# Attention resumes at the first unfinished step: absent parts of a batch's first chunk count as done

## The chip, the core and the metric

The kernel runs on one core of a Trainium2 chip. The metric is the time of one execution on the device in microseconds (us). TensorE is called PE here, VectorE DVE, ScalarE ACT, GpSimd POOL and SyncE SP.

## What is computed

Three layers follow each other: a gated linear attention with a running state per head, a dense two-layer MLP, and a mixture of eight experts of which each token takes one.

```python
# attention: 4 batches, 8 heads, 768 steps, head size 40
m_new = np.maximum(f_gate[:, :, t] + m, i_gate[:, :, t])
C = f_stab[:, :, None, None] * C + i_stab[:, :, None, None] * np.einsum('bhd,bhe->bhde', vt, kt)
h_tilde = np.einsum('bhde,bhe->bhd', C, qt)
denom = np.maximum(np.abs(nq), 1.0)
y[:, :, t] = o * h_tilde / denom
# dense layer: 3072 tokens, 320 -> 2048 -> 320
x = (np.maximum(x @ w_in, 0.0) ** 2) @ w_out
# routed layer: 8 experts, 320 -> 1024 -> 320, gate_w from a softmax
out[mask] = gate_w[mask, None] * (np.maximum(x[mask] @ w1[e], 0.0) @ w2[e])
```

## The kernel before

**Attention in chunks.** The sequence of each batch is cut into 6 chunks of 128 steps (`c` is the chunk's place in its batch, 0 to 5), 24 chunks in all. Chunks 0 to 2 are the first ones (c = 0) of batches 0 to 2; then come chunks 3 to 7 (batch 0, c = 1 to 5), 8 to 12 (batch 1), 13 to 17 (batch 2) and 18 to 23 (batch 3). A chunk's work is a list of named parts in nine steps (`STEPS`): scores q·k (`scores`, L775), the product of q with the carried state C (`inter`, L715), the weighting by decays (`weigh0`, `weigh1`, L780), the products with v (`values0`, `values1`, L788), the new state (`update`, L715, and `update_masked`, `carried`, L811 to L819), the division, the gate, and a transpose into the layout of the dense layer (`turned`, L724). For c = 0 there is no carried state, so `inter`, `scaled` and `carried` issue nothing there.

**Loads and preparation.** `prepare(n, h)` runs ahead of a chunk: loads of kvo (L616), of q and k (`st`, L629, 960 KB a chunk, two buffers), of decays (L650), all on SP's queue; the rounding of q and k (ACT L640, POOL L643, four pieces a half) and the causal mask of the decays (POOL L671, L672).

**Dense layer in groups.** Three chunks are a group of 384 tokens; there are 8 groups. Each group takes 16 iterations (f): eight matmuls of layer 1 (L866) and nine of layer 2 (L899 to L901). Layer 1 runs two iterations ahead of layer 2. A group's sums leave PSUM at L981; `fin` then computes the experts' logits of that group (L955, L964) and writes the tokens out (L1059, on SP) in steps, one an iteration.

**What sets the order.** The order is written by the program that builds the kernel. First it goes through a list of words, `PLAN`, that interleaves the attention of chunks 0 to 6, the decoding of the dense weights and the first iterations, one word at a time. The list ends after layer 1 of iteration 17 and layer 2 of iteration 15, that is at the end of group 0, with chunks 0 to 6 through all their parts. Behind it a loop over iterations takes over. Each iteration calls `attend` twice; `attend` adds 0.7 to a counter and for each whole number runs one `half` step: the due tail step (`rest`), the next step of `steps[0]` (six a chunk, `PERIOD`) and its `prepare`. A part that is in `done` is not issued again. `half` stops at `evac(first[g1 + 2])`, a limit of two groups ahead. Before layer 1 of a new group, `until` runs all `half` steps at once that this group still needs.

**Where the loop starts.** `catch_up` moves `steps[0]` past the steps whose parts are all in `done`, and calls `prepare` for them. `PLAN` has no word for `inter`, `scaled` and `carried` of chunks 0 to 2, so step 0 of chunk 0 is never finished by that test, and `steps[0]` stays 0. The loop then spends 42 half steps (7 chunks of 6) on parts that are all done.

Of the kernel before, what the change touches and what calls it, by code (L numbers as in the profile page):

```python
# [373 lines left out]
def kernel(ctx, tc, qk, q3, kvo, gates, w_io, wg, w12, cst, out, dbg=None):  # L374
# [361 lines left out]
    class Main:  # L736
# [18 lines left out]
                self.run(part)  # L755

        def finished(self, k):
            return all(part in self.done for part in self.STEPS[k])

        def inter(self):  # L760
            d = self.d
# [788 lines left out]
```

## Time and profile before

| | us |
|---|---|
| median of 3 runs (824.13 to 825.09) | 824.89 |
| the profiled execution | 822.93 |
| its span, first to last instruction | 821.1 |
| PE busy in the span | 777.9 |
| DVE, ACT, POOL busy | 503.5, 407.7, 384.8 |
| group 1, from the end of group 0 to its own | 84.27 |
| groups 2, 3, 4, 5 | 65.35, 65.63, 60.45, 63.41 |
| groups 6, 7 | 50.76, 48.97 |

A group's time is read between the starts of its and the preceding group's evacuation (L981). Busy times of PE are of pipelined matmuls whose ends are modelled. A page has 40 slices of 20.5 us; the granted clock of PE is 1.00 at 2.4 GHz and 0.50 at 1.2 GHz. The profiled execution took 1.96 us less than the median.

### The profile page before, as it was taken

The page shows a single profiled execution, that of the slowest core. Times are in us where ns is not written, and L with a number is a line of the kernel's source. Part 1 is how long each engine was busy: PE and PEld are TensorE (multiplying, and loading weights), DVE is VectorE, ACT ScalarE, POOL GpSimd, SP SyncE. Part 2 cuts the span into 40 slices and gives each one's busy share as a digit, 9 for nine tenths or more (in the row PEclk, how much of TensorE's full clock was granted, in tenths as well). Part 3 has the DMA queues.
Part 4 walks back from the last instruction along what each step waited for, and adds up shares of the span by engine and source line. Part 5 has one row for each costly group of instructions (what it writes and reads, how often), then busy time and mean ns, then how long its engine had stood idle before and what let it go on. Part 6 is the DMA issues. An engine that isn't in the chain of part 4 may idle for free.

```text
span 821.1 us, 14163 instructions
## 1 busy us (share of the span) xinstructions
PE 777.9 (95%) x5120; PEld 753.8 (92%) x5120; DVE 503.5 (61%) x1102; ACT 407.7 (50%) x760; POOL 384.8 (47%) x430
## 2 busy tenths in 40 slices
PE   7999999995899989999999999999989999999996
PEld 5789989995899989899999999999989999999996
DVE  6358998454458567748558655444527555886553
ACT  2346766332445544454454543454327544876553
POOL 5238997017555665554454410142044533465551
PEclk9999999995799999999999999999989999999998
DMA  8257861046485445454343400010048666777520
GB/s 260 79 159 220 235 177 31 1 135 169 111 269 151 122 117 149 107 141 122 87 121 109 143 1 31 2 47 13 31 126 303 197 184 181 206 248 231 192 70 32
DMA packets 55046, 109.03 MB, mean 133 GB/s; under 512 B 6896, under 2 KB 34681, under 8 KB 54834
## 3 DMA queue, kind: packets, MB, share of 16 engines
q1 hardware_dynamic: 50370, 95.88, 40.1%
q0 software_dynamic: 4160, 11.77, 4.4%
q8 instruction: 48, 0.79, 0.4%
q10 hardware_dynamic: 432, 0.29, 0.1%
q14 instruction: 36, 0.29, 0.1%
HBM read 98.69 MB, written 10.86 MB: 133 GB/s over the span
## 4 chain that ended last, share of the span: by engine, by line
PE 63%; POOL 8%; DVE 8%; DMA 6%; issue 3%; ACT 1%; SPq 1%; DVEq 0%; POOLq 0%; ACTq 0%
PE hp L866 16%; PE hp L288 12%; DMA st<-in_qk_dram 6%; PE acc L899 5%; PE acc L901 5%; PE acc L900 5%; PE op L308 3%; PE op L307 3%; PE op L309 3%; POOL kq L643 3%; PE pv L788 2%; POOL Ab L671 2%; PE lp L964 1%; PE xp L274 1%; PE tp L715 1%
## 5 line engine op out<-in xcount | busy, mean ns | idle before, releaser
L643 POOL TENSOR_TENSOR kq<-st,kq 120x256 fp32r<-120x256 f32 x136 | 100.3, 769 | 101.7 <-ACT kq L640 90.1
L899 PE MATMUL acc<-w_h,gh 128*128 128x320 f32 x384 | 125.7, 327 | 0.0
L901 PE MATMUL acc<-w_h,gl 128*128 128x320 f32 x384 | 120.0, 313 | 1.5 <-POOL gl L886 1.4
L866 PE MATMUL hp<-xh,w_h 128*128 128x384 f32 x384 | 114.4, 352 | 5.9 <-ACT scr L959 2.0
L900 PE MATMUL acc<-w_l,gh 128*128 128x320 f32 x384 | 119.3, 311 | 0.0
L874 ACT ACTIVATE g<-hp 128x384 f32<-128x384 f32 x128 | 62.0, 484 | 105.5 <-PE hp L866 104.9
L883 DVE SCALAR_TENSOR_TENSOR hp<-hp,g 128x384 f32<-128x384 f32 x121 | 67.7, 559 | 66.5 <-ACT g L874 66.3
L257 DVE SCALAR_TENSOR_TENSOR gl<-hp,gh 128x384 fp32r<-128x384 f32 x88 | 47.1, 553 | 71.2 <-ACT gh L227 59.3
L866 PE MATMUL hp<-xh,w_l 128*128 128x384 f32 x384 | 89.0, 340 | 0.2 <-POOL w_l L582 0.2
L866 PE MATMUL hp<-xl,w_h 128*128 128x384 f32 x256 | 87.8, 343 | 0.0
L886 DVE TENSOR_TENSOR gl<-hp,gh 128x384 fp32r<-128x384 f32 x121 | 67.5, 558 | 13.4 <-DVE hp L883 0.5
L901 PEld LDWEIGHTS acc<-w_h,gl 128*128 128x128 f32 x384 | 73.0, 190 | 2.0 <-POOL gl L886 1.7
L866 PEld LDWEIGHTS hp<-xh,w_h 128*128 128x128 f32 x384 | 66.8, 192 | 8.2 <-ACT scr L959 2.3
L899 PEld LDWEIGHTS acc<-w_h,gh 128*128 128x128 f32 x384 | 73.3, 191 | 0.1
L900 PEld LDWEIGHTS acc<-w_l,gh 128*128 128x128 f32 x384 | 73.4, 191 | 0.0
L866 PEld LDWEIGHTS hp<-xh,w_l 128*128 128x128 f32 x384 | 70.2, 191 | 0.5 <-POOL w_l L582 0.5
L875 ACT ACTIVATE gh<-g 128x384 fp32r<-128x384 f32 x128 | 67.2, 525 | 6.0 <-PE acc L900 2.0
L227 ACT ACTIVATE gh<-hp 128x384 fp32r<-128x384 f32 x88 | 42.6, 491 | 44.9 <-PE hp L288 43.6
L678 ACT ACTIVATE Ab<-Ab 128x512 f32<-128x512 f32 x42 | 26.2, 628 | 70.8 <-POOL Ab L672 70.7
L640 ACT ACTIVATE kq<-st,cs 120x1024 fp32r<-120x1024 f32 x34 | 38.9, 1145 | 44.6 <-DMA st<-in_qk_dram 42.7
L684 POOL TENSOR_TENSOR vw<-kvo,wT 128x378 f32<-128x378 f32 x20 | 17.2, 858 | 86.5 <-DMA kvo<-in_kvo_dram 36.1
L788 PEld LDWEIGHTS pv<-kvo,Ab 128*128 128x128 f32 x384 | 55.5, 218 | 1.6 <-DVE Ab L780 1.5
(273 smaller groups left out, 1929.2 us busy)
## 6 DMA issues: line engine op xcount, KB each, us to landing
st<-in_qk_dram SPq DMA_DIRECT2D x34, 480.0 KB
raw<-in_w_dram SPq DMA_DIRECT2D x30, 512.0 KB
kvo<-in_kvo_dram SPq DMA_DIRECT2D x24, 529.0 KB
raw<-in_w_io_dram SPq DMA_DIRECT2D x16, 704.0 KB
Ab<-A_d SPq DMA_DIRECT2D x42, 256.0 KB
raw<-in_w_dram SPq DMA_DIRECT2D x20, 427.0 KB
raw<-in_w_dram SPq DMA_DIRECT2D x10, 426.0 KB
q<-in_q_dram SPq DMA_DIRECT2D x20, 180.0 KB
```

Of the source, the lines that this page charges most:

```text
L257: e.scalar_tensor_tensor(out=gl[:, j], in0=hp[j % 4], scalar=0.0, in1=gh[:, j].bitcast(F32), op0=ALU.max, op1=ALU.subtract).then_inc(sGL, 1)
L288: m = e.matmul(hp[f % 4][:, 0:w], a, c, start=(n == 0), stop=(n == 7))
L643: nc.gpsimd.tensor_tensor(out=o[:, c], in0=self.st[j][:, c], in1=o[:, c].bitcast(F32), op=ALU.subtract)
L788: nc.tensor.matmul(self.pv[:, hd], d.Ab[r][:, i], d.v[:, hd], start=True, stop=True)
L866: nc.tensor.matmul(hp, a, x, start=(n == 0), stop=(n == 7))
L874: nc.scalar.activation(out=r, in_=hp, func=ACTF.Relu)
L875: nc.scalar.activation(out=gh, in_=r, func=ACTF.Square)
L883: e.scalar_tensor_tensor(out=sq, in0=hp, scalar=0.0, in1=r, op0=ALU.max, op1=ALU.mult)
L886: e.tensor_tensor(out=gl, in0=sq, in1=gh.bitcast(F32), op=ALU.subtract)
L899: nc.tensor.matmul(acc[t][:, 0:DM], gh[:, sl], wh, start=(f == 0), stop=False)
L900: nc.tensor.matmul(acc[t][:, 0:DM], gh[:, sl], wl, start=False, stop=False)
L901: nc.tensor.matmul(acc[t][:, 0:DM], gl[:, sl], wh, start=False, stop=end)
```

## The change

`finished` takes `inter`, `scaled` and `carried` as done where c is 0. `catch_up` then moves `steps[0]` on to the first step that has something left.

```diff
@@ -755,7 +755,7 @@
         def finished(self, k):
-            return all(part in self.done for part in self.STEPS[k])
+            return all(part in self.done or (self.c == 0 and part in ("inter", "scaled", "carried")) for part in self.STEPS[k])
```

No instruction's form or operands change; the order does. On PE, behind the end of `PLAN` in group 1, the first two rows of chunk 7 (`tp<-C` is `inter`, `sp<-kq` is `scores`) now stand in the first iteration of the loop:

```order
 L866 MATMUL hp<-xl,w_h 128x384
 L866 MATMUL hp<-xh,w_l 128x384 x3
+L715 MATMUL tp<-C,q_1096 128x126 x3
+L775 MATMUL sp<-kq 128x128 x8
 L955 MATMUL lpt<-cs,xr_81 128x128 x3
 L899 MATMUL acc<-w_h,gh 128x320
```

Chunks 8 and 9 follow in later iterations of group 1 in the same way. Before, PE has these three chunks in one block between the last layer-1 products of group 1 and the first of group 2 (q_1096, q_1758 and q_1815 are the q of chunks 7, 8 and 9):

```order
L901 MATMUL acc<-w_h,gl 128x320
L715 MATMUL tp<-C,q_1096 128x126 x3
L775 MATMUL sp<-kq 128x128 x8
L788 MATMUL pv<-kvo,Ab 128x42 x8
L715 MATMUL tp<-C,q_1758 128x126 x3
L775 MATMUL sp<-kq 128x128 x8
L724 MATMUL xpt<-cs,kvo 128x128 x3
L715 MATMUL tp<-vw,kvo 120x126 x3
L788 MATMUL pv<-kvo,Ab 128x42 x8
L715 MATMUL tp<-C,q_1815 128x126 x3
L775 MATMUL sp<-kq 128x128 x8
L724 MATMUL xpt<-cs,kvo 128x128 x3
```

This block is gone from that place. On SP's queue, the loads of chunks 8, 9 and 10 now stand ahead of the writes of group 0's tokens (`x_d`); before, those of chunk 8 came behind them. SP, from the loads of chunk 9 on (q_1441 and q_1671 are the q of chunks 9 and 10 in the changed kernel):

```order
+L650 DMA Ab<-A_d 128x4x128 x2
+L616 DMA kvo<-in_kvo_dram 128x1058
+L629 DMA st<-in_qk_dram 120x1024 x2
+L633 DMA q_1441<-in_q_dram 120x384
+L650 DMA Ab<-A_d 128x4x128 x2
+L616 DMA kvo<-in_kvo_dram 128x1058
+L629 DMA st<-in_qk_dram 120x1024 x2
+L633 DMA q_1671<-in_q_dram 120x384
 L1059 DMA x_d<-xr_81 128x392 x3
 L650 DMA Ab<-A_d 128x4x128 x2
-L629 DMA st<-in_qk_dram 120x1024 x2
-L633 DMA q_1758<-in_q_dram 120x384
```

What moved is when SP may ask for q and k: the writes no longer stand in front of chunks 8 to 10.

Attention matmuls by group, counted from the order on PE between the last layer-2 products of one group and of the next (matmuls of `scores`, of `inter` and `update` together, of `values`, of `turned`; one call of a part is 8, 3, 4 and 3 matmuls):

| group | before | after |
|---|---|---|
| 1 | 24, 15, 24, 6 | 32, 21, 28, 9 |
| 2 | 32, 21, 24, 12 | 24, 15, 28, 9 |
| 3 | 24, 18, 32, 9 | 24, 18, 24, 9 |
| 4 | 24, 12, 24, 9 | equal |
| 5 | 24, 18, 24, 9 | equal |
| 6 | 8, 3, 8, 6 | equal |
| 7 | 0, 0, 0, 9 | equal |

## Rows read from the trace of the kernel before

**Rows 1.** The page: span, and slices of PE and its clock.
```profile
span 821.1 us, 14163 instructions
PE   7999999995899989999999999999989999999996
PEclk9999999995799999999999999999989999999998
```

**Rows 2.** Windows, groups 1 to 7: stretch, length, busy times (count), PEclk, DMA, GB/s.
```profile
136.30:220.57 84.27, 71.84 (x423) 69.25 (x422) 40.65 (x109) 30.99 (x60) 32.37 (x49) 0.80 0.32 87
220.57:285.92 65.35, 63.33 (x445) 61.88 (x443) 44.51 (x110) 33.39 (x67) 34.27 (x48) 1.00 0.64 190
285.92:351.55 65.63, 62.01 (x434) 60.64 (x434) 46.05 (x111) 31.91 (x64) 37.62 (x51) 1.00 0.44 120
351.55:412.00 60.45, 59.35 (x416) 58.66 (x415) 37.50 (x94) 30.21 (x60) 30.10 (x42) 1.00 0.43 117
412.00:475.41 63.41, 60.27 (x420) 59.10 (x419) 42.08 (x103) 30.62 (x61) 31.46 (x43) 1.00 0.42 119
475.41:526.17 50.76, 50.76 (x343) 50.52 (x342) 27.74 (x80) 20.26 (x45) 0.77 (x4) 1.00 0.04 13
526.17:575.14 48.97, 48.97 (x355) 48.62 (x353) 22.83 (x71) 24.11 (x49) 18.35 (x15) 1.00 0.08 26
```

**Rows 3.** Windows inside group 1, same columns.
```profile
136.30:178.40 42.10, 42.10 (x280) 41.69 (x279) 23.30 (x74) 16.78 (x36) 3.12 (x11) 1.00 0.19 56
178.40:210.60 32.20, 19.78 (x94) 17.59 (x93) 13.24 (x30) 10.74 (x17) 20.95 (x28) 0.56 0.55 145
210.60:220.57 9.97, 9.96 (x51) 9.97 (x52) 4.11 (x7) 3.47 (x8) 8.31 (x11) 0.72 0.14 29
200.00:210.00 10.00, 4.48 (x19) 3.61 (x18) 2.83 (x8) 2.56 (x6) 4.31 (x6) 0.50 0.75 190
217.00:219.00 2.00, 2.00 (x16) 2.00 (x15) 0.00 (x0) 0.00 (x0) 1.93 (x3) 1.00 0.40 75
```

**Rows 4.** Timeline of PE in the block: start, length, instruction, idle before, releaser.
```profile
186.68 2.74 PE L775 MATMUL sp<-kq 120*128 120x128 f32 x8 [1.80 <-POOL kq L643]
193.03 0.88 PE L724 MATMUL xpt<-cs,kvo 128*128 128x128 f32 x3 [3.61 <-DVE kvo L840]
205.60 0.88 PE L724 MATMUL xpt<-cs,kvo 128*128 128x128 f32 x3 [3.61 <-DVE kvo L840]
210.61 0.98 PE L866 MATMUL hp<-xh,w_h 128*128 128x384 f32 x2 [1.72 <-DVE xh L734]
```

**Rows 5.** Waits of SP's queue, 120 to 230 us: total, times, longest.
```profile
SPq L1059 <- DVE xr L1055: 40.9, 1, 40.9
```

**Rows 6.** Chain that ended last, full clock: start, length, attention products.
```profile
218.44 0.82 PE pv L788 x8
223.70 0.67 PE tp L715 x6
224.37 0.85 PE sp L775 x8
226.68 0.33 PE xpt L724 x3
```

**Rows 7.** The same chain: from a chunk's loads to its last mask, twice.
```profile
273.09 0.37 SPq L650
...
292.00 0.65 POOL Ab L672
...
310.39 0.39 SPq L650
...
329.98 0.65 POOL Ab L672
```

**Rows 8.** Waits, 220 to 480 us, and PE's longest idle time there.
```profile
ACT kq L640 <- DMA st<-in_qk_dram: 37.2, 11, 6.5
421.78 0.62 PE L866 MATMUL hp<-xh,w_h 128*128 128x384 f32 x2 [1.44 <-ACT scr L959]
```

## The prediction

> **What bounds the kernel now.** I read the page first: its slices of PE and of the granted clock [rows 1]. PE is at 9 nearly everywhere, so the kernel is bound by PE, with one clear exception: the tenth and eleventh slice (about 185 to 226 us) show PE at 5 and 8 tenths and the clock at 5 and 7. The second view is the windows by group [rows 2]. Group 1 takes 84.27 us, groups 2 to 5 take 60.45 to 65.63. The third is the same view inside group 1 [rows 3]. From 136.30 to 178.40 PE is busy all of 42.10 us at full clock, with POOL at 3.12 and DMA at 0.19: this is the dense layer alone, while the loop spends its half steps on chunks that are done. From 178.40 to 210.60 PE is busy 19.78 of 32.20 us at a mean clock of 0.56: this is the block of chunks 7, 8 and 9, which `until` issues at once. From 210.60 to 220.57 PE is busy, but at 0.72.
>
> The fourth view is the timeline of the block [rows 4]. PE stands 1.80 us for the rounding of q and k, twice 3.61 us for the end of the chunk before (DVE L840) and 1.72 us for the columns of group 2. In the block nothing lies beside these chains of load, rounding, mask, weighting and division, because no dense product is left to issue. The clock goes down with it: it is 0.50 (1.2 GHz) in the stretch 200 to 210 with PE busy 4.48 of 10 us, and 1.00 (2.4 GHz) again in 217 to 219 [rows 3].
>
> **The change, part by part.** *What PE must do.* The change adds and removes no products on PE; it moves them. I price them at full clock [rows 6]: a call of scores 0.85 us, of `inter` or `update` 0.67, of `values` 0.82, of `turned` 0.33. The dense part of a group comes from group 6, which holds little attention: 50.76 us [rows 2], less one call of scores, one of `inter`, two of `values` and two of `turned` (0.85 + 0.67 + 1.64 + 0.66 = 3.82), is 46.94 us.
>
> Before, by the counts of the change's table: group 1 has 3 scores, 5 products with the state, 6 values, 2 turned: 2.55 + 3.35 + 4.92 + 0.66 = 11.48, with the dense part 58.4 us. Groups 2 to 5 come to 61.3, 61.1, 58.1 and 59.4 in the same way. Against the measured 84.27, 65.35, 65.63, 60.45 and 63.41 [rows 2] the excess is 25.9 in group 1 and 4.1, 4.6, 2.4 and 4.0 in the others.
>
> After: group 1 has 4, 7, 7, 3 calls (3.40 + 4.69 + 5.74 + 0.99 = 14.8), 61.8 us; group 2 has 3, 5, 7, 3, 59.6 us; group 3 has 3, 6, 6, 3, 59.4 us. The sum of groups 1 to 3 is 180.8 us in both kernels; it is the excess that differs.
>
> *What the excess becomes.* Before it is 25.9 + 4.1 + 4.6 = 34.6 us in these three groups. In groups 2 to 5 the loop already runs as it will in group 1: steps of a chunk between dense products. Their mean excess is 3.7 us, from 2.4 to 4.6. I take it for each of the three groups after, 11.2 us with the decimals kept. The gain is 34.6 - 11.2 = 23.4 us. With 2.4 a group it is 27.4, with 4.6 a group 20.8.
>
> *What hides the moved work.* The DVE, ACT, POOL and DMA work of chunks 7 to 9 then lies beside group 1's dense products. In 136.30 to 178.40 DVE is busy 23.30, ACT 16.78 and POOL 3.12 of 42.10 us [rows 3], so there is room; over a whole group DVE would come to the 46 of 65.6 us that group 3 shows [rows 2]. Were that cover gone, the block's excess would come back, 25.9 - 3.7 = 22.2 us.
>
> *The queue of SP.* Before, SP stands 40.9 us for group 0's tokens (L1059 waits for DVE L1055) [rows 5], and the loads of chunk 8 stand behind it. After, the loads of chunks 8 to 10 come first. That is needed for the gain: chunk 8's scores now fall in group 1. The writes themselves come later. Their buffer is written again only at the end of group 2, a group's 65 us away, and the rows are read after group 5; I cost them at nothing. Behind them now stand kvo of chunk 10 and the decays, q and k of chunk 11. The writes' DVE part is issued in about the eleventh iteration of group 1, and so are these loads (15 half steps at 1.4 an iteration), so the wait should be short. The bounds are 0 and one iteration, about 65/16 = 4 us; I take 0, since in groups 2 to 5 the queue has the same order and its cost is in their 3.7.
>
> *POOL, ACT, DVE.* They run the same operations in another order. POOL, nearly idle while the dense layer runs alone and the feeder of the block behind it [rows 3], works through the whole group. Nothing is priced here beyond the excess. Nor are groups 4 to 7 and the routed layer: their order is the same, they start earlier, and PE is what they wait for.
>
> The sum: 822.93 us for the profiled execution less 23.4 is 799.5. The median stands 1.96 us above that execution, so on the median it is 824.89 - 23.4 = 801.5 us.
>
> **The rivals.** *First, the clock falls inside group 1 as well.* The block shows what a fall costs: a gap of 3.61 us [rows 4], and from 210.61 on, with PE busy, some 6.4 us at half speed until it is full in the window that starts at 217 [rows 3], so 3.2 us lost: 6.8 us a fall. One fall gives 808.3, two 815.1 us. Against it: groups 2 to 5 have 13 chunks' scores between dense products and show 1.00 throughout [rows 2], and PE's longest idle time there is 1.44 us [rows 8]. If each of the four calls of scores in group 1 brought a fall, it would be 4 x 6.8 = 27.2 us, 828.7 us in all; this decides from 23.4/6.8 = 3.4 falls on. I give it 1 in 100, and one or two falls 9 in 100. The Trainium skill, page "TensorE: Matmul & The Clock Gate", section "HAM oscillation — how this bites in real kernels", speaks against the change here: it describes a kernel whose waits for data return in each pass of its loop and put the clock down in each, so that the cost is paid every time and not once. By that rule the one fall of the block would become one for each chunk, the 828.7 us; the trace does not bear it out, since the clock row of groups 2 to 5 shows no fall.
>
> *Second, on the slower side: the chain of loads sets the pace.* The next q and k can be loaded only when the last have been rounded (two buffers), and ACT stands in its order until they land: 37.2 us in 11 waits [rows 8], with the dense ReLU behind it, and PE behind that. From a chunk's decay load to its last mask the chain takes 273.09 to 292.65, 19.6 us, and 310.39 to 330.63, 20.2 us [rows 7]. Group 1 takes 14 iterations of 1.4 half steps, 19.6 steps or 3.27 chunks. At 20.2 us a chunk that is 66.1 us, as much as the 61.8 + 3.7 = 65.5 that PE would take; the chain just fits. At 24 us a chunk group 1 would take 78.5, and the kernel 814.5 us. It is slower than before only from (65.5 + 23.4)/3.27 = 27.2 us a chunk on; at 30 us a chunk, with DMA, SP and POOL all late for each, it would be 834. For it: DMA is at 0.75 of its 16 engines in the window from 200 to 210 us, where the block waits for its loads [rows 3]; against it: 20 us is measured with the same loads in flight. 3 in 100 for slower, 8 in 100 for a loss of 5 to 13 us in this way.
>
> *Third, nothing changes:* the loop would reach the same limits by group 2 and lose what it gained, 824.9 us. The limit `evac` lets attention run two groups ahead, and before it is caught up by group 3 in any case; so the products move within groups 1 to 3 only. But what is gained is PE's idle and half-speed time, and it would have to come back as new idle time in a later group whose order is the same. 3 in 100.
>
> *Fourth, more than forecast:* the excess of groups 2 and 3 was the block's aftermath, and all three groups come to their products alone, 34.6 us less, 790.3. Group 5, far behind the block, still has 4.0; 4 in 100.
>
> **How the numbers follow.** The forecast of 801.5 us (797.5 to 804.1 with the bounds of the excess) has 72 in 100; one or two falls 9, a chain that costs 5 to 13 us 8, nothing 3, more 4, slower 3 + 1. The range from 796.5 to 810 holds the forecast, one fall, and the smaller losses of the chain, some 83 in 100. A difference of 0.2% (1.65 us) is about what a measurement of this kernel can tell from none. Faster by more: 72 + 9 + 8 + 4 = 93 in 100; within: 3; slower by more: 4.
>
> **What would show it.** In the profile after, the page's slices have no fall of PE's clock near 200 us. Windows between the evacuations show group 1 at about 65 us with a clock of 1.00, groups 2 and 3 at 63 us each, and groups 4 to 7 as they were within a microsecond. SP's wait for L1059 is far below 40.9 us. Scores of chunks 7, 8 and 9 lie some 17 us apart from about 138 us on. I am wrong in the size if group 1's excess is outside 2 to 5 us, wrong in the mechanism if a clock below 1.00 stands in group 1, and wrong in the cover if ACT's waits for q and k there are longer than the 3.4 us each (37.2/11) of the later groups.

## The result, and the profile after

The changed kernel takes 802.97 us in the median (801.30 to 804.73), against 824.68 of the kernel before: 0.9737 of it, 95% interval 0.9714 to 0.9761. It is 21.7 us faster; 801.5 was forecast, with a gain of 23.4. The profiled execution, 804.73 us, is the slowest of its four. The page of that execution, with its slices of PE and of the clock (compare [rows 1]):

```profile
span 802.9 us, 14148 instructions
PE   7999998989899999999999999999989998998996
PEclk9999999999999999999999999999999999999999
```

The fall of PE and of its clock at the tenth and eleventh slice is gone. The windows between the evacuations, with the columns of [rows 2]: group 1, 2, 3, 4, 5 and 7, and one wait of SP in 120 to 230 us (total, times, longest):

```profile
135.42:205.63 70.21, 66.80 (x466) 65.65 (x465) 48.58 (x123) 33.91 (x65) 39.44 (x58) 0.98 0.42 121
205.63:267.94 62.31, 59.65 (x417) 58.89 (x416) 41.57 (x101) 31.10 (x62) 33.64 (x47) 1.00 0.60 172
267.94:328.99 61.05, 59.55 (x419) 58.89 (x418) 43.11 (x106) 30.66 (x62) 31.14 (x43) 1.00 0.43 119
328.99:390.29 61.30, 59.61 (x416) 58.61 (x415) 37.74 (x94) 30.00 (x61) 30.11 (x42) 1.00 0.40 115
390.29:453.99 63.70, 60.26 (x420) 59.07 (x419) 42.08 (x103) 30.63 (x61) 31.47 (x43) 1.00 0.41 119
...
504.76:553.73 48.97, 48.97 (x354) 48.63 (x353) 22.84 (x71) 24.14 (x48) 18.33 (x15) 1.00 0.08 26
```
```profile
SPq L1059 <- DVE pb L1066: 6.5, 1, 6.5
```

Group 1 went from 84.27 to 70.21 us, group 2 from 65.35 to 62.31, group 3 from 65.63 to 61.05. Groups 4 to 7 are as they were within 0.9 us. SP's wait for the writes of group 0 is 6.5 us in place of 40.9 [rows 5]. Of the spans' difference, 18.2 us, the three groups give 21.7 and the start 0.9; groups 4 and 5 take 1.1 back, and the part behind group 7 took 3.2 us more, 249.17 for 245.96. That last part has the same order in both kernels, and in the twelve profiles below it lies between 244.1 and 254.1 whatever was changed ahead of it, so its 3.2 us are put down to the execution, not to the change.

A window ends where ACT begins the evacuation, and in group 1 of the changed kernel ACT comes late to it. The last layer-2 product of group 1 begins on PE at 203.88 us; ACT waits 1.93 us for a mask until 204.16 and begins the evacuation at 205.63:

```profile
135.95 0.31 PE L901 MATMUL acc<-w_h,gl 128*128 128x320 f32 x1
...
203.88 0.31 PE L901 MATMUL acc<-w_h,gl 128*128 128x320 f32 x1
...
204.16 0.63 ACT L678 ACTIVATE Ab<-Ab 128x512 f32<-128x512 f32 x1 [1.93 <-POOL Ab L672]
...
205.63 1.07 ACT L981 ACTIVATE xrl<-acc 128x320 f32<-128x320 f32 x3
```

Between the last layer-2 products of group 0 (135.95) and of group 1 (203.88) PE itself takes 67.93 us; in the kernel before this is 83.52 us (136.82 to 220.34). Below, "by PE's products" means this second reading. The three groups together come to the same gain by it, 21.7 us.

What is not as forecast is inside group 1. PE stands there once, and the clock falls behind it. The timeline of PE (start, length, instruction, idle before) and four windows with the columns above:

```profile
173.30 1.12 PE L775 MATMUL sp<-kq 120*128 120x128 f32 x8
176.86 0.83 PE L866 MATMUL hp<-xh,w_h 128*128 128x384 f32 x2 [2.44 <-DVE gl L886]
```
```profile
174.00:176.00 2.00, 0.42 (x4) 0.28 (x3) 1.86 (x8) 0.52 (x1) 0.00 (x0) 1.00 0.97 259
...
178.00:180.00 2.00, 2.00 (x9) 2.00 (x8) 0.88 (x2) 0.36 (x1) 0.00 (x0) 0.50 0.66 231
...
182.00:184.00 2.00, 2.00 (x16) 2.00 (x15) 1.69 (x5) 2.00 (x4) 2.00 (x4) 1.00 0.02 4
...
176.86:182.00 5.14, 5.14 (x23) 5.13 (x24) 3.11 (x14) 2.31 (x4) 0.30 (x2) 0.67 0.51 175
```

PE is without work from about 174.4 to 176.86 us; from 178 to 180 it is busy at 1.2 GHz, from 182 on at 2.4 GHz. Over the 5.14 us from 176.86 to 182 the mean clock is 0.67, so about 1.7 us are lost there (5.14 x 0.33); with the gap, the fall costs about 4.1 us. What stood ahead of it is read from ACT and from DVE, whose timelines are in the experiments.

### The profile page after: what moved, and what is told of

Read it like the earlier page. It is cut to its first block, busy times and chain, and to the rows that moved or that the text cites. A ratio compares the mean times of both kernels' runs of the same rounds, so it can differ in the third digit from the quotient of the medians.

```text
span 802.9 us, 14148 instructions
## 1 busy us (share of the span) xinstructions
PE 765.6 (95%) x5120; PEld 743.2 (93%) x5120; DVE 508.6 (63%) x1102; ACT 407.5 (51%) x760; POOL 388.0 (48%) x430
## 4 chain that ended last, share of the span: by engine, by line
PE 68%; DVE 11%; POOL 9%; issue 5%; DMA 4%; ACT 2%; DVEq 0%; SPq 0%; POOLq 0%; ACTq 0%
PE hp L866 16%; PE hp L288 11%; PE acc L899 5%; PE acc L901 5%; PE acc L900 5%; DMA st<-in_qk_dram 4%; PE pv L788 4%; PE op L308 3%; PE op L307 3%; PE op L309 3%; POOL kq L643 3%; PE sp L775 2%; PE tp L715 2%; POOL Ab L671 2%; PE Ap L662 1%
## 5 line engine op out<-in xcount | busy, mean ns | idle before, releaser
L643 POOL TENSOR_TENSOR kq<-st,kq 120x256 fp32r<-120x256 f32 x136 | 100.4, 770 | 72.6 <-ACT kq L640 70.2
L866 PE MATMUL hp<-xh,w_h 128*128 128x384 f32 x384 | 114.7, 353 | 7.0 <-DVE gl L886 4.8
L874 ACT ACTIVATE g<-hp 128x384 f32<-128x384 f32 x128 | 62.0, 484 | 91.3 <-PE hp L866 90.9
L883 DVE SCALAR_TENSOR_TENSOR hp<-hp,g 128x384 f32<-128x384 f32 x121 | 67.5, 558 | 51.3 <-ACT g L874 51.2
L866 PE MATMUL hp<-xh,w_l 128*128 128x384 f32 x384 | 88.6, 338 | 0.3 <-POOL w_l L582 0.2
L866 PE MATMUL hp<-xl,w_h 128*128 128x384 f32 x256 | 87.6, 342 | 0.0
L866 PEld LDWEIGHTS hp<-xh,w_h 128*128 128x128 f32 x384 | 66.1, 191 | 8.9 <-DVE gl L886 5.6
L866 PEld LDWEIGHTS hp<-xh,w_l 128*128 128x128 f32 x384 | 69.6, 190 | 0.9 <-POOL w_l L582 0.9
L170 POOL DMA_INDIRECT out_dram<-ot,idx x34 | 41.4, 1217 | 28.2 <-ACT ot L206 20.8
```

The source lines that it names most:

```text
L643: nc.gpsimd.tensor_tensor(out=o[:, c], in0=self.st[j][:, c], in1=o[:, c].bitcast(F32), op=ALU.subtract)
L866: nc.tensor.matmul(hp, a, x, start=(n == 0), stop=(n == 7))
L874: nc.scalar.activation(out=r, in_=hp, func=ACTF.Relu)
L883: e.scalar_tensor_tensor(out=sq, in0=hp, scalar=0.0, in1=r, op0=ALU.max, op1=ALU.mult)
```

## Experiments

Groups are read from evacuation to evacuation where nothing else is said. Ratios are to the kernel before, measured beside each run, with their 95% intervals.

### Is it the empty half steps, and how many?

The kernel before, with the counter set by hand behind `catch_up`:

```diff
         catch_up()
+        steps[0], tails[:] = 21, (3, 0)
```

> The kernel before, with the loop's step counter set to 21 in place of 0 behind the list of words (half of the 42 empty half steps are skipped). Theory (what counts is how many useful half steps lie in group 1): its 19.6 half steps are then still all empty (21 to 40.6), the block of chunks 7 to 9 stays whole, and the time stays at 824.5 us within 1.5. Rival (the gain goes with the number of empty steps skipped): half of 21.7 us, about 814 us.

It took 823.42 us in its one execution, against 824.94 of the kernel before, within the 1.5 us of the theory. Half of the empty steps were skipped, and the gain of some 11 us that the rival asked for is not there.

```diff
         catch_up()
+        steps[0], tails[:] = 33, (5, 0)
```

> The kernel before, with the step counter set to 33: 9 empty half steps and then about 10 useful ones, so chunks 7 and 8 go beside group 1's dense products and only chunk 9 is left for the block. Theory (each chunk in the block costs its own wait for load, rounding and division at half clock): two of three chunks' cost goes, the block shrinks from 32 to 8 to 12 us, and the time is 808 to 813 us. Rival (the cost is the drop of the clock and the start of the block, whatever its length): 818 to 823 us.

813.44 us, ratio 0.9842 (0.9807 to 0.9877), just above the theory's 808 to 813 and below the rival's 818 to 823. The two windows of group 1, from 21 and from 33:

```profile
135.12:219.93 84.81, 70.30 (x429) 67.98 (x428) 40.13 (x109) 31.01 (x59) 32.39 (x49) 0.82 0.33 88
```
```profile
137.80:209.79 71.99, 64.62 (x430) 62.92 (x428) 42.18 (x106) 30.65 (x60) 31.00 (x44) 0.93 0.33 90
```

Group 1 is 84.81 us where all its half steps are still empty, and 71.99 where two of the three chunks of the block lie beside the dense products. The gain follows the chunks that leave the block, not the steps that are skipped. With one chunk left in the block, the clock is 0.93 in place of 0.80. Not all of the 12.3 us of group 1 stayed in the total: group 3 took 67.30 us here, 1.7 more than before, with a clock of 0.97.

### The queue of SP alone

```diff
         catch_up()
+        for i in range(PERIOD * WHOLE):
+            prepare(*divmod(i, PERIOD))
```

> The kernel before, with only the preparation that is asked for behind the list of words moved up: decays, q and k of chunk 8 stand ahead of group 0's writes on SP's queue, and attention still begins with 42 empty half steps. Theory (the queue's order is a condition of the gain and no gain in itself): chunk 8's q and k had landed before the block began anyway, so 824.5 us within 1.5. Rival (the block's waits come from loads that stood behind the writes): 3 us or more faster.

824.35 us, ratio 0.9982 (0.9963 to 1.0002); group 1 took 84.08 us. The early loads are no gain by themselves. In the kernel before, ACT began to round chunk 8's q and k at 180.21 us and had waited for PE, not for the load, so they had landed. That the early loads are a condition of the gain is argued from the order, since chunk 8's scores now fall in group 1; no run has the change without them.

### Stand or half clock?

```diff
         while steps[0] <= evac(n):
             half(n + 1)
+            if n == 8 and steps[0] > PERIOD * WHOLE:
+                p = psa.tile([128, 512], F32, tag="a", name="dummy")
+                for _ in range(4):
+                    nc.tensor.matmul(p, ones, ones.rearrange("p (o n) -> p o n", o=1).to_broadcast([128, 4, 128]), start=True, stop=True)
```

> The kernel before, with four matmuls on constants (128x512, read by nobody) behind each of the 15 useful half steps of the block, some 0.2 us each at full clock, so that PE is busy through the block's waits. It separates the two halves of the 25.9 us excess: 12.4 us in which PE stood, 13.5 us of half clock. Theory (the chains of load, rounding and division set the block's length, and the half clock costs mainly behind it, 3.2 us, and a part of its products): 3 to 8 us faster, 817 to 822 us, the block still 26 us or longer. Rival (the half clock is the larger half and is all lost time): 11 us or more faster, below 814 us.

824.36 us, ratio 0.9995 (0.9977 to 1.0014): neither. The windows of group 1 and of the block, and PE's timeline from the block's first product to the end of group 1; then three rows of the same timeline in the kernel before, where group 2's first product is at 210.61 [rows 4]:

```profile
135.17:221.93 86.76, 78.84 (x490) 68.55 (x488) 41.43 (x109) 30.98 (x59) 32.48 (x49) 0.94 0.32 90
...
177.34:212.00 34.66, 27.85 (x154) 18.29 (x153) 13.44 (x29) 10.63 (x17) 21.05 (x28) 0.85 0.48 135
```
```profile
177.34 0.83 PE L715 MATMUL tp<-C,q 120*128 120x126 f32 x6
...
178.86 2.77 PE L1190 MATMUL dummy<-ones 128*128 128x512 bf16 x12
181.46 0.98 PE L788 MATMUL pv<-kvo,Ab 128*128 128x42 f32 x8
...
192.43 0.87 PE L724 MATMUL xpt<-cs,kvo 128*128 128x128 f32 x3 [3.47 <-DVE kvo L840]
...
202.24 1.09 PE L775 MATMUL sp<-kq 120*128 120x128 f32 x8
...
212.00 0.59 PE L866 MATMUL hp<-xh,w_h 128*128 128x384 f32 x2 [0.64 <-DVE xh L734]
...
219.12 0.31 PE L901 MATMUL acc<-w_h,gl 128*128 128x320 f32 x1
...
222.40 0.55 PE L955 MATMUL lpt<-cs,xrl 128*128 128x128 f32 x3 [1.58 <-ACT xrl L981]
```
```profile
178.44 0.83 PE L715 MATMUL tp<-C,q 120*128 120x126 f32 x6
...
199.97 2.03 PE L775 MATMUL sp<-kq 120*128 120x128 f32 x8
...
220.34 0.31 PE L901 MATMUL acc<-w_h,gl 128*128 128x320 f32 x1
```

The clock's mean over group 1 rose from 0.80 to 0.94 and over the block from 0.56 to 0.85, and the time stayed. Two things cancel. The block, from chunk 7's first product to group 2's, became longer, 34.7 us (177.34 to 212.00) for 32.2 (178.44 to 210.61). Behind it the stretch to group 1's last layer-2 product became shorter, 7.1 us (212.00 to 219.12) for 9.7 (210.61 to 220.34), as its clock is full; PE then stood 1.58 us for the evacuation, to which ACT came late. So behind the block the half clock did cost PE 2.6 us. What it costs in the block this run cannot tell: twelve of the products on constants take 2.6 us of PE (178.86 to 181.46), all sixty by this estimate some 13, and part of that stands ahead of the block's own products. Chunk 9's scores begin 24.9 us after the block's start, for 21.5 before. A stand of 3.47 us for the end of a chunk (L840) is still there, so at least this wait does not come from the clock alone.

### What made group 1 longer than forecast?

The changed kernel again, as the base of the next three:

> The changed kernel again, as the base of the next three on the same chip: 801 to 805 us, and group 1 at about 70 us with one gap of PE near its eleventh iteration, if that gap belongs to the kernel and not to one execution.

801.40 us, ratio 0.9716 (0.9685 to 0.9747). The same gap returned: 2.44 us in front of L866, at 177.45, and group 1 took 69.84. By PE's products it took 67.95 us, and 67.93 in the execution above. The gap belongs to the kernel.

**The small operations of group 0 on DVE.** DVE is busy 1.86 of 2 us in the gap, and near it stand the update of chunk 8's state and nine small operations in a row, without a break. From the timeline of DVE, changed kernel:

```profile
167.34 0.97 DVE L819 TENSOR_TENSOR C<-C,U 120x378 f32<-120x378 f32 x1
168.22 0.15 DVE L1013 COPY mc<-ep 128x8 f32<-128x8 f32 x1
...
170.68 0.18 DVE L1025 TENSOR_TENSOR oh<-rot,ei 128x24 bf16<-128x24 f32 x1
170.78 0.18 DVE L1027 TENSOR_TENSOR ex<-lg,mx 128x24 f32<-128x24 f32 x1
171.70 0.57 DVE L883 SCALAR_TENSOR_TENSOR hp<-hp,g 128x384 f32<-128x384 f32 x1 [0.74 <-ACT g L874]
```

```diff
             counts(ep, True, True, *[(slice(0, 1), on[:, t:t + 1]) for t in range(n)])
             yield
+            yield
+            yield
             mc = rw.tile([128, 8], F32, tag="mc", name="mc")
```

> The changed kernel, with the nine small DVE operations that find group 0's most frequent expert (L1013 to L1025, 2.5 us in a row) and all that follows them two iterations later, away from the update of chunk 8's state (L811 to L819). Theory (group 1's excess of 8.4 us in place of 3.7 comes from DVE being late there, with PE's gaps and the clock's fall behind it): 3 to 5 us faster than the changed kernel, no clock below 1.00 in group 1. Rival (the chain of loads and roundings, which the chain of waits shows in group 1, sets it): within 1 us of the changed kernel.

800.47 us, ratio 0.9707 (0.9678 to 0.9736), and group 1 took 69.62 us with a gap of 2.14. The theory fell: these operations alone were not what PE waited for. The last row above points to the reason: when DVE came to L883 it waited 0.74 us for ACT.

**ACT's order.** The timeline of ACT in the changed kernel, and the layer-1 products on PE that the ReLU at 171.19 us takes up:

```profile
165.54 0.63 ACT L678 ACTIVATE Ab<-Ab 128x512 f32<-128x512 f32 x1 [0.52 <-POOL Ab L672]
170.65 0.63 ACT L678 ACTIVATE Ab<-Ab 128x512 f32<-128x512 f32 x1 [4.49 <-POOL Ab L672]
171.19 0.47 ACT L874 ACTIVATE g<-hp 128x384 f32<-128x384 f32 x1
```
```profile
167.02 0.68 PE L866 MATMUL hp<-xh,w_l 128*128 128x384 f32 x3
```

ACT stands 4.49 us for chunk 9's second mask, the end of a chain that began with a load at 152.21, and the dense ReLU (L874) stands behind it in ACT's order: its products end at 167.70, and it begins 3.5 us later. The edit puts the two exponentials one step later:

```diff
-3: [(n + 2, "decays"), (n + 1, "causal", 1), (n + 1, "decay", 0)],
-4: [(n + 1, "decay", 1)], 5: [(n + 1, "weighted")]}
+3: [(n + 2, "decays"), (n + 1, "causal", 1)],
+4: [(n + 1, "decay", 0)], 5: [(n + 1, "decay", 1), (n + 1, "weighted")]}
```

> The changed kernel, with the two exponentials of the next chunk's decays (ACT L678) asked for one step later, so that the dense ReLU (L874) of that iteration stands ahead of them in ACT's order. Theory (group 1's excess comes from ACT standing in its order for the end of the chain load, rounding, mask, 4.5 us at 166 us, with the dense ReLU and then PE behind it): the gap of 2.4 us and the fall of the clock go, group 1 at 65 to 68 us, the kernel 3 to 6 us faster than the changed one. Rival (DVE is what is late in group 1, whatever ACT does): group 1 at 69 to 71 us, within 1.5 us.

796.59 us, ratio 0.9667 (0.9638 to 0.9696). ACT's waits in group 1, changed kernel and this one (total, times, longest), and this one's windows of groups 1 and 4 and its gap:

```profile
ACT Ab L678 <- POOL Ab L672: 15.0, 7, 4.5
```
```profile
ACT g L874 <- DVE C L818: 2.8, 1, 2.8
...
ACT Ab L678 <- POOL Ab L672: 0.9, 2, 0.4
```
```profile
135.53:202.35 66.82, 64.35 (x449) 63.47 (x448) 46.84 (x121) 33.80 (x65) 37.84 (x56) 0.97 0.42 124
...
323.68:381.87 58.19, 57.96 (x409) 57.53 (x408) 36.88 (x94) 30.06 (x59) 30.17 (x42) 1.00 0.43 119
```
```profile
176.12 0.62 PE L866 MATMUL hp<-xh,w_h 128*128 128x384 f32 x2 [1.56 <-DVE gl L886]
```

ACT's wait for the masks went from 15.0 to 0.9 us, group 1 from 69.84 to 66.82, group 4 from 60.65 to 58.19. The kernel is 4.8 us under the changed one's 801.40, or 4.0 us by the two ratios, which is the theory in time. But the gap did not go: 1.56 us of it are left, and the clock falls to 0.50 behind it again. By PE's products group 1 went only from 67.95 to 66.82 us; the other 1.9 us are ACT's lateness at the evacuation. Now ACT waits for DVE (L818), which is late next.

**Both together.**

> The exponentials one step later and the nine small DVE operations of group 0 two iterations later, together. Theory (with ACT's stand gone, DVE is what is late next, near 170 us: the update of the state and the nine operations in a row): now moving them pays what it did not pay alone; the gap of 1.6 us that was left goes, the clock is 1.00 in group 1, group 1 at 64 to 66 us in place of 66.8, the kernel 1 to 3 us under the one with late exponentials alone (796.6). Rival (the gap that is left hangs on the attention of chunk 9 itself): within 1 us of it.

796.44 us, ratio 0.9640 (0.9623 to 0.9657); the late exponentials alone took 796.59, with a ratio of 0.9667. By the medians nothing is added; by the ratios it would be 2.2 us, which the intervals do not separate from none. Two windows at the place of the old gap, group 1, and the gap that it has now:

```profile
174.00:178.00 4.00, 4.00 (x30) 4.00 (x29) 3.64 (x16) 1.13 (x3) 0.82 (x1) 1.00 0.97 244
...
135.96:203.16 67.20, 64.56 (x449) 63.46 (x448) 48.79 (x121) 33.70 (x65) 39.46 (x59) 0.97 0.44 123
```
```profile
194.82 0.84 PE L724 MATMUL xpt<-cs,kvo 128*128 128x128 f32 x3 [1.75 <-DVE kvo L840]
```

At 174 to 178 us PE is now busy throughout, as the theory wanted, but a stand of 1.75 us came up at 194.82 and the group is as long as with the late exponentials alone. Here lateness that was taken from one place showed in the next.

**The loads ahead of the decays.**

```diff
-QK0, QK1, ROUND0, ROUND1 = 1, 3, (3, 4), (1, 2)
+QK0, QK1, ROUND0, ROUND1 = 1, 2, (3, 4), (1, 2)
```

> The changed kernel, with q and k of the chunk after next asked for one step earlier, ahead of the decays and kvo on SP's queue, in which they wait for buffers that come free later. Theory (the chain of loads is late in group 1, and its start is held by the decays' buffers): q and k land 2 to 5 us earlier, group 1 at 65 to 69 us, the kernel 2 to 5 us faster than the changed one. Rival (the transfers are in time, and what is late is the rounding and masking on POOL, or DVE): within 1.5 us.

796.79 us, ratio 0.9667 (0.9638 to 0.9697): in all what the theory wanted. ACT no longer waits for loads of q and k in group 1 (4.0 us in the changed kernel, 7.2 in its second execution) and still waits up to 4.4 us for a mask. By the evacuations group 1 took 69.02 us, 0.8 less; by PE's products 66.25 for 67.95, since ACT comes late to the evacuation here too. The largest gain lies in group 5, 60.57 for 63.72. So the transfers are late in the later groups as well, and in group 1 the waits for the masks stay. These groups come from an execution of 803.33 us, the slowest of its six, whose part behind group 7 is the longest of all, 254.1 us.

### Less attention for each dense product

```diff
-STEP = 0.7
+STEP = 0.6
```

> The changed kernel with 0.6 in place of 0.7 half steps a call: 16.8 half steps in group 1 in place of 19.6, so less attention for each dense product, and the same total by group 6. Theory (the excess comes where DVE cannot follow the density of attention): group 1 at 62 to 65 us, the kernel 2 to 5 us faster. Rival (each chunk costs its own excess wherever it stands): within 1 us.

792.09 us, ratio 0.9603 (0.9570 to 0.9637): 9.3 us under the changed kernel measured beside it, more than the theory had. Its group 1:

```profile
135.78:197.50 61.72, 60.79 (x432) 59.94 (x431) 41.55 (x113) 30.72 (x60) 32.15 (x49) 1.00 0.43 120
```

DVE has 41.55 us in group 1 in place of 49.00, POOL 32.15 in place of 39.52, the clock is 1.00, and the group is 8.1 us shorter, 6.2 by PE's products, with only half a chunk less in it. No later group pays more than 0.5 us for it: 62.36, 60.44, 60.01, 63.06 and 51.21 us for 62.11, 60.81, 60.65, 63.72 and 50.77.

> The changed kernel with 0.57 half steps a call, just over the 18 a group that the dense layer needs: attention reaches into group 6, where the kernel has little of it. Theory (density): another 0 to 2 us faster than with 0.6. Rival (each chunk its own excess): no difference to 0.6; or the last chunk of a group comes too late for layer 1, and a small block of one or two steps returns before each group, 1 to 4 us slower than with 0.6.

The edit is the same line with 0.57. 792.16 us, ratio 0.9615 (0.9589 to 0.9642), no difference to 0.6 that can be told. Groups 2 to 5 are 1.0 to 2.0 us shorter than with 0.6, and group 6 is 54.12 us for 51.21: the attention moved there.

> The changed kernel with 0.57 half steps a call and the exponentials one step later. It asks whether the two remedies take away the same stands. Theory (both remove ACT's and DVE's lateness in the same iterations): little is added, 789 to 792 us. Rival (they act on different stands): 5 us more than 0.57 alone (792.2), 787 us or less.

With 0.57 and the late exponentials 792.05 us, ratio 0.9593 (0.9568 to 0.9617). Nothing that can be told is added, which fits the theory that both take away the same stands. These three, 31 to 33 us under the kernel before, are the fastest versions seen here, and 0.6 alone is the smallest edit to the changed kernel that gets there.

## Why the prediction was right, and where it was not

**The block's excess: right.** The step that carried the sum was that group 1's excess over its products falls to what the other groups have. The total of groups 1 to 3 was forecast as 180.8 + 11.2 = 192.0 us and came out as 193.57. The runs with the counter at 21 and 33 show the mechanism: it is chunks 7 to 9 leaving the block that pays. (With two decimals kept all through, the prediction's own sum is 34.5 - 11.3 = 23.2.)

**The excess in group 1: the term that was mis-sized.** It was put at 3.7 us, with 2.4 to 4.6 as bounds; it measured 70.2 - 61.8 = 8.4, and 67.9 - 61.8 = 6.1 by PE's products. What stands in its place is one fall of the clock, which the forecast had left to its first rival: some 4.1 us, the gap of 2.44 and 1.7 lost at half speed behind it. That is more than the 2.4 us by which 6.1 lies above 3.7. Groups 2 and 3 had 62.3 - 59.6 = 2.7 and 61.1 - 59.4 = 1.7, less than the 3.7 (3.8 and 2.3 by PE's products). The errors went against each other: 12.8 us for the three where 11.2 was said. That the total came within 1.5 us of the forecast is therefore in part luck.

The step that did not hold is "the loop already runs there as it will in group 1". It runs there against its limit (`evac`) for part of each group; in group 1 it begins 20 half steps short of it and does all 19.6, with group 0's extra work on DVE beside them. That the pace matters is borne out by the runs with 0.6 and 0.57; moving group 0's extra work alone gained nothing that can be told. Which engine's lateness comes first stays open: ACT, DVE and the loads each moved part of it. By the words of the prediction itself, the size was wrong (excess outside 2 to 5), the mechanism was not the whole one (a clock below 1.00 in group 1), and the cover was not whole either (ACT's one wait for q and k was 4.0 us, above 3.4).

**The first rival came in part.** One fall of the clock was there, with a gap of 2.44 us and 1.7 us lost behind it, where 3.61 and 3.2 were counted. It did not come with each chunk: four calls of scores, one fall. The section "HAM oscillation — how this bites in real kernels" of the page "TensorE: Matmul & The Clock Gate" in the Trainium skill, on waits that return in each pass and put the clock down in each, is not borne out here beyond that one.

**The second rival named a mechanism that was there, at a smaller size.** The chain of load, rounding and mask did hold ACT in its order and the dense ReLU behind it, for 4.49 us at one place. The late exponentials took that away and gained 3.0 us in group 1 by the evacuations, 1.1 by PE's products. I had said that ACT's waits for q and k would show it; they were 4.0 us, once, and the waits for the mask were 15.0. Loads one step earlier gained 1.7 us there by PE's products. Neither is the whole: with 0.6 ACT still waits in group 1 for q and k (7.2 us) and for masks (5.2 us), and the clock does not fall.

**The half clock as lost time: borne out behind the block, open in it.** The first rival's price counts time at half speed as half lost. Behind the block the products on constants brought back 2.6 us of the 3.2 that it counted. In the block no run shows what the half clock costs.

**The rest.** The writes behind the loads cost nothing that shows; SP stood 6.5 us for them, more than the 4 given as the bound. Scores of chunks 7 to 10 lie at 139.2, 157.0, 173.3 and 194.1 us, 16 to 21 apart where 17 was said. Groups 4 to 7 kept their times.

## What to carry to other kernels

A scheduler's counter that waits for work that does not exist holds back all that stands behind it and then lets it out in one block, where there is nothing left to hide it; count the calls that issue nothing. What is spread out again has a best pace: here that of the limits (18 half steps a group), or just above it, was better than a faster one, and 0.7 gave back 9 us that 0.6 kept. A wait in an engine's order is paid by what stands behind it: read ACT's waits by what comes next on ACT, not only by the engine that is waited for. And a window that ends at one engine's work holds that engine's lateness too: read the busiest engine's own products beside it.

## What was not expected of the hardware

Keeping PE busy with products on constants through the block raised its granted clock from 0.56 to 0.85 and moved the time by nothing that can be measured (0.9995). That does not show the half clock to be free: PE's stretch behind the block was 2.6 us shorter, and the block with the constants in it 2.5 us longer.

The length of PE's idle time alone does not tell whether the clock falls. It fell to 0.50 behind 1.56 us (late exponentials, 176.12) and behind 1.75 us (both together, 194.82), and it stayed at 1.00 behind 1.76 us in group 5 of the changed kernel. Late exponentials, then the changed kernel:

```profile
178.00:180.00 2.00, 2.00 (x9) 2.00 (x8) 1.65 (x4) 1.84 (x3) 0.00 (x0) 0.50 0.59 209
```
```profile
400.39 0.62 PE L866 MATMUL hp<-xh,w_h 128*128 128x384 f32 x2 [1.76 <-ACT scr L959]
...
400.39:406.00 5.61, 5.61 (x39) 5.58 (x39) 5.04 (x10) 3.72 (x7) 5.54 (x9) 1.00 0.05 14
```

The part behind group 7, the same in all these kernels, took between 244.1 and 254.1 us in the profiles, while the groups of the changed kernel's two profiles lie within 1 us of each other. A few microseconds between two executions can come from there alone.
